# Sixteen tokens of one head in each partition of the q and k tiles, in a fused attention and feed-forward kernel

## The chip, the core and the metric

The kernel runs on one core of a Trainium2 chip. The metric is device time in microseconds (us) from launch to end; it is given as the median of several runs. One further execution was recorded by the hardware profiler, and all readings of engines, queues and waits come from that one.

## The reference

`q`, `k` and `v` are float32 of shape (8 batches, 8 heads, 576 tokens, 64). Attention is local: each chunk of 64 tokens attends to itself alone. The result, with the heads side by side, is a (4608, 512) matrix `x`, which goes through a multiplicative feed-forward.

```
chunk = 64;  scale = 1 / sqrt(64)
scores = scale * q_c @ k_c^T            # per batch, head and chunk: 64 x 64
attn   = softmax(scores)
out    = attn @ v_c                     # -> x: (4608, 512)
a = x @ w1;  b = x @ w2                 # (512 -> 1024) each
h = (a * b) @ w3                        # (1024 -> 1024)
result = h @ w_out                      # (1024 -> 512), float32
```

The kernel multiplies `w3` and `w_out` once (steps V, W, Z below) and then uses only the product `w3o`.

## The kernel before

The 4608 tokens are cut into 18 parts of 256 tokens (four chunks of 64; part number `p`), and two parts make a group of 512 (`g = p // 2`). All matmuls are in bf16. `ORDER` is one long string that writes out by hand the order of all steps; each step is a letter with its part and further numbers, and each engine runs its own steps strictly in that order. The letters that matter here:

- `R0`, `R1`: load `q` and `k` of part 0 as float32 (`raw`) on the queues of SyncE and ScalarE. `K0`, `K1`: ScalarE casts them to bf16.
- `q5`, `k5`, `v5` and so on: load part 5 with a cast from float32 to bf16 in the DMA. These, and all weights (`i0` to `i3` are quarters of `w1` and `w2`, `o` is `w_out`, `h0`, `h1` are halves of `w3`), are issued by GpSimd (POOL) on one queue, in the order of the string.
- `T p.s`: VectorE (DVE) transposes `q` (s=0) or `k` (s=1) of part `p`, in blocks of 32 x 32, from the tile `qk` to the tile `qkT` (line 201).
- `S`: scores on TensorE (PE) (64 small matmuls). `E`: exp on ScalarE. `P`: the product with `v` on PE (64 small matmuls). The tile `vbuf` holds a column of ones beside `v`, so the row sums come with it.
- `N p.u`: reciprocal and scaling on DVE. `X p.u`: transpose to `xt` (or `xm` from part 8 on) on DVE (lines 297, 305).
- `A`, `B` p.j: the products with `w1` and `w2` on PE. `C`: ScalarE copies A's result to SBUF. `M`: DVE multiplies (line 366).
- `O`, `Y`, `Q`: output product on PE, copy on ScalarE, store on SyncE's queue. `G`, `H`: from part 8 on, SBUF to SBUF moves on SyncE's queue.
- `D which.p.j.n.cols`: `n` matmuls of zeros over `cols` columns into a PSUM tile that is written properly afterwards.

PE's matmuls are all issued through one helper (line 95), POOL's loads through another (line 98), SyncE's moves through a third (line 193). PSUM is a pool of four tiles of two banks each; `qk` tiles have five buffers and `qkT` tiles two.

In `qk`, before, a partition of a 32-partition block holds two consecutive tokens of each of the 8 heads: per head a run of 2 x 64 float32 = 512 B in memory, 256 B in bf16. A block of 32 partitions is one chunk. The transpose writes, inside each 32 x 32 block, 32 elements that lie two elements (4 B) apart.

Of the kernel before, what the change touches and what calls it, by code (L numbers as in the profile page):

```python
# [7 lines left out]

ORDER = """
R0 R1 v0 q1 k1 i0 v1 i1 i2 q2 k2 v2 i3 q3 k3 v3 q4 k4 v4 o h0 h1 D0.0.0.16.64 K0 T0.0 K1 T0.1 q5 k5  # L10
v5 S0 T1.0 E0 P0 D0.1.0.4.512 T1.1 q6 k6 v6 N0.0 S1 D1.0.0.5.512 X0.0 N0.1 X0.1 A0.0 E1 B0.0 C0.0 P1
M0.0 A0.1 N1.0 X1.0 B0.1 C0.1 N1.1 A0.2 X1.1 B0.2 C0.2 M0.1 A1.0 T2.0 B1.0 C1.0 M0.2 A1.1 T2.1 q7 k7
v7 B1.1 C1.1 M1.0 S2 M1.1 A0.3 E2 T3.0 B0.3 C0.3 P2 M0.3 A1.2 N2.0 X2.0 B1.2 C1.2 N2.1 A1.3 X2.1
B1.3 C1.3 M1.2 A2.0 T3.1 q8 k8 v8 B2.0 C2.0 M1.3 S3 T4.0 A2.1 E3 M2.0 B2.1 T4.1 q9 k9 C2.1 P3 v9
M2.1 A2.2 N3.0 B2.2 C2.2 X3.0 A2.3 N3.1 B2.3 X3.1 C2.3 M2.2 S4 M2.3 A3.0 E4 B3.0 C3.0 A3.1 M3.0 B3.1
C3.1 V0 A3.2 M3.1 B3.2 C3.2 V1 A3.3 M3.2 B3.3 C3.3 V2 W0 M3.3 V3 W1 Z0 V4 V5 W2 Z1 V6 V7 T5.0 Z2 W3
T5.1 q10 k10 T6.0 T6.1 P4 v10 q11 k11 Z3 S5 N4.0 O0 E5 X4.0 N4.1 X4.1 T7.0 O1 T7.1 Y0 Q0 T8.0 P5 v11
q12 k12 Y1 S6 T8.1 O2 Q1 E6 N5.0 X5.0 N5.1 X5.1 O3 T9.0 T9.1 Y2 G4.0 P6 v12 q13 k13 A4.0 N6.0 B4.0
G4.1 Y3 X6.0 N6.1 C4.0 A4.1 X6.1 B4.1 C4.1 M4.0 Q2 S7 Q3 M4.1 A4.2 E7 T10.0 B4.2 C4.2 T10.1 P7 v13
q14 k14 A4.3 M4.2 B4.3 N7.0 C4.3 A4.4 X7.0 M4.3 B4.4 C4.4 N7.1 A4.5 M4.4 B4.5 C4.5 X7.1 S8 M4.5 S9  # L20
E8 A4.6 T11.0 B4.6 E9 T11.1 P8 v14 q15 k15 C4.6 A4.7 M4.6 G5.0 B4.7 C4.7 N8.0 A6.0 M4.7 B6.0 N8.1
C6.0 G5.1 A6.1 X8.0 B6.1 M6.0 C6.1 X8.1 P9 v15 A6.2 M6.1 N9.0 B6.2 C6.2 N9.1 A6.3 M6.2 B6.3 C6.3
X9.0 A6.4 M6.3 B6.4 C6.4 X9.1 A6.5 T12.0 H4.0 B6.5 C6.5 M6.4 A6.6 M6.5 B6.6 T12.1 H4.1 C6.6 S10 S11
M6.6 E10 A6.7 T13.0 B6.7 E11 P10 T13.1 C6.7 O4 M6.7 G6.0 N10.0 N10.1 X10.0 G6.1 P11 Y4 X10.1 O5
N11.0 N11.1 x11 q16 k16 v16 Q4 X11.0 X11.1 T14.0 A8.0 H5.0 Y5 B8.0 T14.1 C8.0 A8.1 M8.0 B8.1 H5.1
C8.1 T15.0 A8.2 B8.2 M8.1 C8.2 T15.1 Q5 A8.3 B8.3 C8.3 M8.2 G7.0 S12 M8.3 S13 E12 A8.4 T16.0 B8.4
E13 G7.1 P12 T16.1 C8.4 A8.5 B8.5 M8.4 C8.5 N12.0 A8.6 M8.5 B8.6 C8.6 N12.1 x12 q17 k17 v17 A8.7
M8.6 B8.7 C8.7 X12.0 P13 M8.7 A10.0 X12.1 B10.0 C10.0 N13.0 A10.1 M10.0 B10.1 N13.1 C10.1 A10.2
X13.0 B10.2 M10.1 C10.2 X13.1 S14 S15 M10.2 E14 A10.3 H6.0 T17.0 B10.3 E15 P14 T17.1 C10.3 A10.4
H6.1 M10.3 B10.4 C10.4 N14.0 A10.5 M10.4 B10.5 G8.0 C10.5 N14.1 A10.6 M10.5 B10.6 C10.6 X14.0 P15  # L30
G8.1 X14.1 A10.7 M10.6 B10.7 N15.0 C10.7 O6 N15.1 M10.7 X15.0 X15.1 H7.0 S16 Y6 S17 O7 E16 E17 H7.1
P16 Y7 O8 Q6 N16.0 Q7 N16.1 X16.0 X16.1 P17 Y8 A12.0 N17.0 Q8 B12.0 N17.1 C12.0 A12.1 X17.0 B12.1
M12.0 C12.1 X17.1 A12.2 M12.1 H8.0 B12.2 C12.2 A12.3 M12.2 B12.3 C12.3 H8.1 A12.4 M12.3 B12.4 C12.4
A12.5 M12.4 B12.5 C12.5 A12.6 M12.5 B12.6 C12.6 A12.7 M12.6 B12.7 C12.7 O9 M12.7 O10 Y9 Q9 A14.0 Y10
B14.0 C14.0 Q10 A14.1 M14.0 B14.1 C14.1 A14.2 M14.1 B14.2 C14.2 A14.3 M14.2 B14.3 C14.3 A14.4 M14.3
B14.4 C14.4 A14.5 M14.4 B14.5 C14.5 A14.6 M14.5 B14.6 C14.6 A14.7 M14.6 B14.7 C14.7 O11 M14.7 O12
Y11 Q11 A16.0 Y12 B16.0 C16.0 Q12 A16.1 M16.0 B16.1 C16.1 A16.2 M16.1 B16.2 C16.2 A16.3 M16.2 B16.3
C16.3 A16.4 M16.3 B16.4 C16.4 A16.5 M16.4 B16.5 C16.5 A16.6 M16.5 B16.6 C16.6 A16.7 M16.6 B16.7
C16.7 O13 M16.7 O14 Y13 Q13 O15 Y14 Q14 O16 Y15 Q15 Y16 Q16 O17
"""  # L40


# [4 lines left out]
def first_path(  # L47
# [41 lines left out]

    def inorder(ins):  # L90
        tc.keep_in_program_order(ins)
        return ins

    def mm(*a, **kw):
        return inorder(nc.tensor.matmul(*a, **kw))  # L95
# [20 lines left out]
    for t in vbuf:  # L116
        inorder(nc.vector.memset(t[:, :, :, D:W], 1.0))
# [12 lines left out]
    qk_t = {}  # L130

    HH = H // 2
    raw_t = {}

    def do_R(s):

        raw_t[s] = msb.tile([P, H, 2 * D], f32, tag="o_sb", name="raw")
        inorder((nc.sync, nc.scalar)[s].dma_start(
            raw_t[s][:], (q, k)[s][0, :, 0:4 * CH, :].rearrange("h (p t) d -> p h (t d)", t=2)))

    def do_K(s):
        if 0 not in qk_t:
            qk_t[0] = io.tile([P, 2, H, 2 * D], bf, tag="qk", bufs=5, name="qk")
        inorder(nc.scalar.copy(qk_t[0][:, s], raw_t[s][:]))  # L144
# [12 lines left out]
    def do_w(p):

# [28 lines left out]
    qkT_t, qkm_t, s_t, e_t, pv_t, xn_t, xm_t, xt_t = {}, {}, {}, {}, {}, {}, {}, {}  # L187
# [7 lines left out]
    def do_T(p, s, h=None):  # L195


        g = p // 2
        if g not in qkT_t:
            qkT_t[g] = asb.tile([P, 2, 2, 2, H, CH], bf, tag="qkT", bufs=2, name="qkT")  # L200
        inorder(nc.vector.transpose(  # L201
            qkT_t[g][:, :, p % 2, s, heads(h)].rearrange("p e h (y t) -> p h t e y", t=2),
            qk_t[p][:, s, heads(h)].rearrange("p h (t e y) -> p h t e y", t=2, e=2)))
# [34 lines left out]
    def do_P(p, hh=None):  # L238
# [183 lines left out]
    def load_q(p, h=None):
        load_qk(p, (0,), h)

    def load_k(p, h=None):
        load_qk(p, (1,), h)
# [6 lines left out]
    def load_half3(i):  # L433
# [134 lines left out]
```

## Time and profile before

| | |
|---|---|
| median of 3 runs | 244.32 us (244.03 to 244.93) |
| the profiled execution's own time | 244.48 us |
| its span, first to last instruction | 242.9 us |
| PE busy | 226.7 us (93%), 2753 matmuls |
| VectorE (DVE) busy | 154.3 us (64%), 235 instructions |
| ScalarE (ACT) busy | 85.2 us (35%) |
| GpSimd (POOL) busy | 83.7 us (34%) |
| POOL's DMA queue | 82592 packets, 18.88 MB |
| read from HBM, written to it | 38.80 MB, 9.44 MB |
| granted TensorE clock | 1.00 |

Busy time is the sum of the instructions on an engine. A window of the profile gives the busy time of each engine in a stretch of the span, with the number of instructions, then the granted clock, the DMA share and the rate at which the DMA engines moved data; for a load with a cast that rate counts the bf16 bytes that are written, half of those that are read. `L201` is line 201 of the kernel.

### The profile page before, as it was taken

The page shows a single profiled execution, that of the slowest core. Times are in us where ns is not written, and L with a number is a line of the kernel's source. Part 1 is how long each engine was busy: PE and PEld are TensorE (multiplying, and loading weights), DVE is VectorE, ACT ScalarE, POOL GpSimd, SP SyncE. Part 2 cuts the span into 40 slices and gives each one's busy share as a digit, 9 for nine tenths or more (in the row PEclk, how much of TensorE's full clock was granted, in tenths as well). Part 3 has the DMA queues.
Part 4 walks back from the last instruction along what each step waited for, and adds up shares of the span by engine and source line. Part 5 has one row for each costly group of instructions (what it writes and reads, how often), then busy time and mean ns, then how long its engine had stood idle before and what let it go on. Part 6 is the DMA issues. An engine that isn't in the chain of part 4 may idle for free.

```text
span 242.9 us, 6385 instructions
## 1 busy us (share of the span) xinstructions
PE 226.7 (93%) x2753; PEld 120.2 (49%) x2753; DVE 154.3 (64%) x235; ACT 85.2 (35%) x116; POOL 83.7 (34%) x114
## 2 busy tenths in 40 slices
PE   1189989999999999999999999999999999999994
PEld 1147868874445444444444444444444444444443
DVE  1756799699799588999998899918540332143000
ACT  2412423423333344425336234162332332322322
POOL 7856976656986345764160230000000000000000
PEclk9999999999999999999999999999999999999999
DMA  6999999999999999999999793735502200400244
GB/s 173 179 185 181 185 169 200 196 193 171 167 173 218 222 228 259 179 224 196 205 236 223 221 139 91 163 88 209 142 0 89 87 0 0 173 3 1 86 173 173
DMA packets 93597, 37.65 MB, mean 155 GB/s; under 512 B 75008, under 2 KB 86528, under 8 KB 93568
## 3 DMA queue, kind: packets, MB, share of 16 engines
q0 software_dynamic: 82592, 18.88, 83.9%
q1 hardware_dynamic: 9936, 17.83, 24.0%
q10 hardware_dynamic: 1040, 0.52, 0.8%
q8 instruction: 21, 0.34, 0.6%
q14 instruction: 8, 0.07, 0.1%
HBM read 38.80 MB, written 9.44 MB: 199 GB/s over the span
## 4 chain that ended last, share of the span: by engine, by line
PE 72%; DMA 16%; DVE 4%; SPq 3%; POOL 2%; issue 1%; ACT 0%; DVEq 0%; POOLq 0%
PE ab_ps L95 39%; PE o_ps L95 23%; PE w_ps L95 6%; DMA w<-in_moe_w_dram 4%; DMA qkm<-qkT 3%; SPq L193 3%; DMA qk<-in_q_dram 3%; DMA qk<-in_k_dram 3%; DMA xt<-xm 3%; PE pv L95 2%; PE s_ps L95 2%; DVE qkT L201 2%; POOL vbuf L98 1%; POOL w L98 1%; DVE xt L297 1%
## 5 line engine op out<-in xcount | busy, mean ns | idle before, releaser
L95 PE MATMUL ab_ps<-xt,w 128*128 128x512 bf16 (+1 forms) x688 | 127.4, 342 | 0.7 <-DVE xt L297 0.6
L95 PEld LDWEIGHTS <-w 128*128 128x128 bf16 x704 | 67.1, 98 | 56.1 <-issue 1.8
L366 DVE TENSOR_TENSOR ab<-a_sb,ab_ps 128x512 bf16<-128x512 f32 x71 | 47.8, 674 | 43.4 <-ACT a_sb L351 43.1
L351 ACT COPY a_sb<-ab_ps 128x512 f32<-128x512 f32 x71 | 41.6, 586 | 81.3 <-PE ab_ps L95 81.0
L95 PE MATMUL o_ps<-w3o,ab 128*128 128x512 bf16 (+1 forms) x296 | 63.9, 373 | 0.0
L201 DVE STREAM_TRANSPOSE qkT<-qk 128x1024 bf16<-128x1024 bf16 x36 | 45.1, 1291 | 7.2 <-ACT qk L144 5.5
L95 PEld LDWEIGHTS <-ab 128*128 128x128 bf16 x296 | 28.5, 98 | 32.2
L98 POOL DMA_DIRECT2D vbuf<-in_v_dram x40 | 33.9, 855 | 20.4 <-DMA qk<-in_q_dram 5.2
L396 ACT COPY o_sb<-o_ps 128x1024 f32<-128x1024 f32 x17 | 17.2, 1012 | 45.3 <-PE o_ps L95 41.3
L264 DVE TENSOR_TENSOR xn<-pv,rcs 128x512 bf16<-128x512 f32 x36 | 24.9, 692 | 1.4
L98 POOL DMA_DIRECT2D qk<-in_q_dram x23 | 18.1, 790 | 8.9 <-DMA qk<-in_k_dram 2.4
L98 POOL DMA_DIRECT2D qk<-in_k_dram x23 | 18.0, 783 | 6.5 <-DMA vbuf<-in_v_dram 3.7
L234 ACT ACTIVATE e<-s_ps 128x1024 bf16<-128x1024 f32 x16 | 15.9, 1026 | 1.7 <-PE s_ps L95 1.3
L95 PE MATMUL w_ps<-wo,w3T 128*128 128x512 bf16 x64 | 14.0, 379 | 0.0
L305 DVE STREAM_TRANSPOSE xm<-xn 128x512 bf16<-128x512 bf16 x20 | 13.5, 696 | 0.2
L261 DVE RECIPROCAL rcs<-pv 128x8 f32<-128x8 f32 x36 | 6.9, 193 | 10.4 <-PE pv L95 10.4
L98 POOL DMA_DIRECT2D w<-in_moe_w_dram x16 | 11.1, 695 | 5.3 <-DMA wo<-in_moe_w_out_dram 2.9
L95 PEld LDWEIGHTS <-e 64*32 64x32 bf16 (+1 forms) x832 | 7.8, 97 | 8.7 <-issue 6.9
L95 PE MATMUL pv<-vbuf,e 64*32 64x65 bf16 (+1 forms) x832 | 10.2, 197 | 1.8 <-ACT e L234 1.1
L297 DVE STREAM_TRANSPOSE xt<-xn 128x512 bf16<-128x512 bf16 x16 | 11.4, 711 | 0.5
L389 DVE COPY o_sb<-o_ps 128x256 f32<-128x256 f32 x1 | 0.4, 425 | 16.0 <-PE o_ps L95 16.0
L95 PEld LDWEIGHTS <-qkT 32*64 32x64 bf16 x512 | 5.5, 117 | 10.1 <-DVE qkT L201 7.9
(29 smaller groups left out, 54.2 us busy)
## 6 DMA issues: line engine op xcount, KB each, us to landing
out_dram<-o_sb SPq DMA_DIRECT2D x17, 512.0 KB, 3.3
qkm<-qkT SPq DMA_DIRECT2D x40, 128.0 KB, 4.0
vbuf<-in_v_dram POOLq DMA_DIRECT2D x32, 128.0 KB, 8.2
w<-in_moe_w_dram POOLq DMA_DIRECT2D x16, 256.0 KB, 9.9
qk<-in_q_dram POOLq DMA_DIRECT2D x11, 256.0 KB, 6.8
qk<-in_k_dram POOLq DMA_DIRECT2D x11, 256.0 KB, 7.8
xt<-xm SPq DMA_DIRECT2D x40, 64.0 KB, 3.2
wo<-in_moe_w_out_dram POOLq DMA_DIRECT2D x4, 256.0 KB, 7.1
```

The source lines that it names most:

```text
L95: return inorder(nc.tensor.matmul(*a, **kw))
L98: return inorder(nc.gpsimd.dma_start(dst, src))
L193: inorder(nc.sync.dma_start(dst, src))
L201: inorder(nc.vector.transpose(qkT_t[g][:, :, p % 2, s, heads(h)].rearrange("p e h (y t) -> p h t e y", t=2), qk_t[p][:, s, heads(h)].rearr ...
L234: inorder(nc.scalar.activation(e_t[p][:, :, heads(hh)], s_t[p][:].rearrange("p u (h q) -> p u h q", q=CH)[:, :, heads(hh)], Exp, scale=sca ...
L261: inorder(nc.vector.reciprocal(rc, pv[:, :, :, D:W]))
L264: inorder(nc.vector.tensor_mul(xn_t[p][:, u], pv[:, :, :, 0:D], rc.to_broadcast([P, 2, 4, D])))
L297: inorder(nc.vector.transpose(new_xt(g)[:].rearrange("p (o t) -> p o t", o=KO)[:, :, t0:t0 + UT] .rearrange("p o (m y) -> p m o y", y=BL), ...
L305: inorder(nc.vector.transpose(xm_t[g][:, u, :, m].rearrange("p o (c y) -> p c o y", y=BL), xn_t[p][:].rearrange("p u r m d -> p (u r) m d" ...
L351: inorder(nc.scalar.copy(a_t[p, j][:], ps_t[p, j][:, 0, :]))
L366: inorder(nc.vector.tensor_mul(o, view(a_t.pop((p, j))[:]), view(ps_t.pop((p, j))[:, 1, :])))
L396: inorder(nc.scalar.copy(o_sb[:], ps_t.pop(p)[:]))
```

## The change

The loads and the transpose of `q` and `k` use another placement, and the steps at the start come in another order.

```
+    RUN = 16
     # do_R: float32 tiles of part 0
-        raw_t[s] = msb.tile([P, H, 2 * D], f32, tag="o_sb", name="raw")
+        raw_t[s] = msb.tile([P, RUN * D], f32, tag="o_sb", name="raw")
-            raw_t[s][:], (q, k)[s][0, :, 0:4 * CH, :].rearrange("h (p t) d -> p h (t d)", t=2)))
+            raw_t[s][:], (q, k)[s][0, :, 0:4 * CH, :].rearrange("h (g t) d -> g h (t d)", t=RUN)))
...
     # load_qk: the casting loads of parts 1 to 17
-                load(qk_t[p][at * BL:(at + m) * BL, s, heads(h)],
-                     (q, k)[s][b, heads(h), c * CH:(c + m) * CH, :].rearrange("h (p t) d -> p h (t d)", t=2))
+                load(qk_t[p][at * BL:(at + m) * BL, s],
+                     (q, k)[s][b, :, c * CH:(c + m) * CH, :].rearrange("h (g t) d -> g h (t d)", t=RUN))
...
     # do_T
-            qkT_t[g][:, :, p % 2, s, heads(h)].rearrange("p e h (y t) -> p h t e y", t=2),
-            qk_t[p][:, s, heads(h)].rearrange("p h (t e y) -> p h t e y", t=2, e=2)))
+            qkT_t[g][:, :, p % 2, s].rearrange("p e h (g t) -> p t e g h", t=RUN),
+            qk_t[p][:, s].rearrange("p (t e y) -> p t e y", t=RUN, e=2)))
```

A block of 32 partitions is still one chunk, but its partitions are now 4 groups of 16 tokens times 8 heads; each holds one run of 16 x 64 float32 = 4 KB in memory, 2 KB in bf16. A load of 128 partitions so has 128 runs instead of 1024. `qkT` is laid out as before, so nothing after the transpose changes; inside a 32 x 32 block the transpose now writes elements that lie one head (64 elements, 128 B) apart, eight of them, then a step of 16 elements (32 B) to the next group.

The order, at the start only (from `M0.0 A0.1 N1.0 ...` on, all steps are as before):

```
before: ... S0 T1.0 E0 P0 D0.1.0.4.512 T1.1 q6 k6 v6 N0.0 S1 D1.0.0.5.512 X0.0 N0.1 X0.1 A0.0 E1 B0.0 C0.0 P1 M0.0 ...
after:  ... S0 T1.0 E0 P0 D0.1.0.4.512 D1.0.0.4.512 N0.0 X0.0 N0.1 X0.1 T1.1 q6 k6 v6 A0.0 B0.0 S1 E1 C0.0 P1 M0.0 ...
```

On DVE, `T1.1` moves behind the four steps `N0.0` to `X0.1`. On PE, `S1` moves behind `A0.0` and `B0.0`, and there is one zero matmul less (4 + 4 instead of 4 + 5), all of them now directly behind `P0`. On POOL the order of the loads stays the same.

More of the change, by code (lines that the diff above doesn't have):

```diff
@@ L9 @@
 ORDER = """
[L10 to L31, printed above, removed]
@@ L32 @@
-P16 Y7 O8 Q6 N16.0 Q7 N16.1 X16.0 X16.1 P17 Y8 A12.0 N17.0 Q8 B12.0 N17.1 C12.0 A12.1 X17.0 B12.1
+R0 R1 v0 q1 k1 i0 v1 i1 i2 q2 k2 v2 i3 q3 k3 v3 q4 k4 v4 o h0 h1 D0.0.0.16.64 K0 T0.0 K1 T0.1 q5 k5 v5
+S0 T1.0 E0 P0 D0.1.0.4.512 D1.0.0.4.512 N0.0 X0.0 N0.1 X0.1 T1.1 q6 k6 v6 A0.0 B0.0 S1 E1 C0.0 P1 M0.0
+A0.1 N1.0 X1.0 B0.1 C0.1 N1.1 A0.2 X1.1 B0.2 C0.2 M0.1 A1.0 T2.0 B1.0 C1.0 M0.2 A1.1 T2.1 q7 k7 v7 B1.1
+C1.1 M1.0 S2 M1.1 A0.3 E2 T3.0 B0.3 C0.3 P2 M0.3 A1.2 N2.0 X2.0 B1.2 C1.2 N2.1 A1.3 X2.1 B1.3 C1.3 M1.2
@@ new lines @@
+A2.0 T3.1 q8 k8 v8 B2.0 C2.0 M1.3 S3 T4.0 A2.1 E3 M2.0 B2.1 T4.1 q9 k9 C2.1 P3 v9 M2.1 A2.2 N3.0 B2.2
+C2.2 X3.0 A2.3 N3.1 B2.3 X3.1 C2.3 M2.2 S4 M2.3 A3.0 E4 B3.0 C3.0 A3.1 M3.0 B3.1 C3.1 V0 A3.2 M3.1 B3.2
+C3.2 V1 A3.3 M3.2 B3.3 C3.3 V2 W0 M3.3 V3 W1 Z0 V4 V5 W2 Z1 V6 V7 T5.0 Z2 W3 T5.1 q10 k10 T6.0 T6.1 P4
+v10 q11 k11 Z3 S5 N4.0 O0 E5 X4.0 N4.1 X4.1 T7.0 O1 T7.1 Y0 Q0 T8.0 P5 v11 q12 k12 Y1 S6 T8.1 O2 Q1 E6
+N5.0 X5.0 N5.1 X5.1 O3 T9.0 T9.1 Y2 G4.0 P6 v12 q13 k13 A4.0 N6.0 B4.0 G4.1 Y3 X6.0 N6.1 C4.0 A4.1 X6.1
@@ new lines @@
+B4.1 C4.1 M4.0 Q2 S7 Q3 M4.1 A4.2 E7 T10.0 B4.2 C4.2 T10.1 P7 v13 q14 k14 A4.3 M4.2 B4.3 N7.0 C4.3 A4.4
+X7.0 M4.3 B4.4 C4.4 N7.1 A4.5 M4.4 B4.5 C4.5 X7.1 S8 M4.5 S9 E8 A4.6 T11.0 B4.6 E9 T11.1 P8 v14 q15 k15
+C4.6 A4.7 M4.6 G5.0 B4.7 C4.7 N8.0 A6.0 M4.7 B6.0 N8.1 C6.0 G5.1 A6.1 X8.0 B6.1 M6.0 C6.1 X8.1 P9 v15
+A6.2 M6.1 N9.0 B6.2 C6.2 N9.1 A6.3 M6.2 B6.3 C6.3 X9.0 A6.4 M6.3 B6.4 C6.4 X9.1 A6.5 T12.0 H4.0 B6.5
+C6.5 M6.4 A6.6 M6.5 B6.6 T12.1 H4.1 C6.6 S10 S11 M6.6 E10 A6.7 T13.0 B6.7 E11 P10 T13.1 C6.7 O4 M6.7
@@ new lines @@
+G6.0 N10.0 N10.1 X10.0 G6.1 P11 Y4 X10.1 O5 N11.0 N11.1 x11 q16 k16 v16 Q4 X11.0 X11.1 T14.0 A8.0 H5.0
+Y5 B8.0 T14.1 C8.0 A8.1 M8.0 B8.1 H5.1 C8.1 T15.0 A8.2 B8.2 M8.1 C8.2 T15.1 Q5 A8.3 B8.3 C8.3 M8.2 G7.0
+S12 M8.3 S13 E12 A8.4 T16.0 B8.4 E13 G7.1 P12 T16.1 C8.4 A8.5 B8.5 M8.4 C8.5 N12.0 A8.6 M8.5 B8.6 C8.6
+N12.1 x12 q17 k17 v17 A8.7 M8.6 B8.7 C8.7 X12.0 P13 M8.7 A10.0 X12.1 B10.0 C10.0 N13.0 A10.1 M10.0 B10.1
+N13.1 C10.1 A10.2 X13.0 B10.2 M10.1 C10.2 X13.1 S14 S15 M10.2 E14 A10.3 H6.0 T17.0 B10.3 E15 P14 T17.1
@@ L33 @@
+C10.3 A10.4 H6.1 M10.3 B10.4 C10.4 N14.0 A10.5 M10.4 B10.5 G8.0 C10.5 N14.1 A10.6 M10.5 B10.6 C10.6
+X14.0 P15 G8.1 X14.1 A10.7 M10.6 B10.7 N15.0 C10.7 O6 N15.1 M10.7 X15.0 X15.1 H7.0 S16 Y6 S17 O7 E16 E17
+H7.1 P16 Y7 O8 Q6 N16.0 Q7 N16.1 X16.0 X16.1 P17 Y8 A12.0 N17.0 Q8 B12.0 N17.1 C12.0 A12.1 X17.0 B12.1
 M12.0 C12.1 X17.1 A12.2 M12.1 H8.0 B12.2 C12.2 A12.3 M12.2 B12.3 C12.3 H8.1 A12.4 M12.3 B12.4 C12.4
@@ L35 @@
 B14.0 C14.0 Q10 A14.1 M14.0 B14.1 C14.1 A14.2 M14.1 B14.2 C14.2 A14.3 M14.2 B14.3 C14.3 A14.4 M14.3
[L36 to L39, printed above, removed]
+B14.4 C14.4 A14.5 M14.4 B14.5 C14.5 A14.6 M14.5 B14.6 C14.6 A14.7 M14.6 B14.7 C14.7 O11 M14.7 O12 Y11
+Q11 A16.0 Y12 B16.0 C16.0 Q12 A16.1 M16.0 B16.1 C16.1 A16.2 M16.1 B16.2 C16.2 A16.3 M16.2 B16.3 C16.3
+A16.4 M16.3 B16.4 C16.4 A16.5 M16.4 B16.5 C16.5 A16.6 M16.5 B16.6 C16.6 A16.7 M16.6 B16.7 C16.7 O13
+M16.7 O14 Y13 Q13 O15 Y14 Q14 O16 Y15 Q15 Y16 Q16 O17
 """
@@ L135, in do_R @@
     def do_R(s):
-        raw_t[s] = msb.tile([P, H, 2 * D], f32, tag="o_sb", name="raw")
+        raw_t[s] = msb.tile([P, RUN * D], f32, tag="o_sb", name="raw")
         inorder((nc.sync, nc.scalar)[s].dma_start(
-            raw_t[s][:], (q, k)[s][0, :, 0:4 * CH, :].rearrange("h (p t) d -> p h (t d)", t=2)))
+            raw_t[s][:], (q, k)[s][0, :, 0:4 * CH, :].rearrange("h (g t) d -> g h (t d)", t=RUN)))
     def do_K(s):
         if 0 not in qk_t:
-            qk_t[0] = io.tile([P, 2, H, 2 * D], bf, tag="qk", bufs=5, name="qk")
+            qk_t[0] = io.tile([P, 2, RUN * D], bf, tag="qk", bufs=5, name="qk")
         inorder(nc.scalar.copy(qk_t[0][:, s], raw_t[s][:]))
@@ L147, in heads, with load_qk @@
         return slice(0, H) if h is None else slice(h * HH, (h + 1) * HH)
-    def load_qk(p, which, h=None):
+    def load_qk(p, which):
         if p not in qk_t:
-            qk_t[p] = io.tile([P, 2, H, 2 * D], bf, tag="qk", bufs=5, name="qk")
+            qk_t[p] = io.tile([P, 2, RUN * D], bf, tag="qk", bufs=5, name="qk")
         for s in which:
             for at, b, c, m in spans(4 * p, 4):
-                load(qk_t[p][at * BL:(at + m) * BL, s, heads(h)],
-                     (q, k)[s][b, heads(h), c * CH:(c + m) * CH, :].rearrange("h (p t) d -> p h (t d)", t=2))
+                load(qk_t[p][at * BL:(at + m) * BL, s],
+                     (q, k)[s][b, :, c * CH:(c + m) * CH, :].rearrange("h (g t) d -> g h (t d)", t=RUN))
     def do_w(p):
@@ L420, in do_Z, with load_q, load_k @@
         inorder(nc.scalar.copy(w3o[:, 2 * m:2 * m + 2, :], ps_t.pop(("w", m))[:]))
[L422 to L426, printed above, removed]
+    def load_q(p):
+        load_qk(p, (0,))
+    def load_k(p):
+        load_qk(p, (1,))
     def load_w12(i):
```

## The prediction

> **What bounds the kernel now.** I read the engine totals first, then the busy time by stretches of the span, then the same for the transposes alone, and last the order of instructions in the first 25 us. In the totals PE is busy for 93% of the span:
>
> ```profile
> PE 226.7 (93%) x2753; PEld 120.2 (49%) x2753; DVE 154.3 (64%) x235; ACT 85.2 (35%) x116; POOL 83.7 (34%) x114
> ```
>
> By stretches (columns: PE, PEld, DVE, ACT, POOL busy, clock, DMA share, GB/s):
>
> ```profile
> 0.00:10.00 10.00, 1.21 (x28) 1.05 (x32) 3.32 (x10) 3.27 (x3) 8.56 (x14) 1.00 1.20 172
> 10.00:25.00 15.00, 12.42 (x320) 8.90 (x315) 9.96 (x17) 3.81 (x5) 9.42 (x13) 1.00 1.75 183
> 25.00:60.00 35.00, 34.05 (x562) 25.85 (x560) 30.46 (x40) 12.65 (x18) 22.81 (x33) 1.00 1.69 187
> 60.00:100.00 40.00, 39.51 (x699) 19.50 (x698) 33.73 (x47) 15.17 (x19) 25.32 (x32) 1.00 1.80 208
> 100.00:150.00 50.00, 49.90 (x592) 23.47 (x590) 46.11 (x73) 20.55 (x30) 17.09 (x23) 1.00 1.40 195
> ```
>
> From 25 us on PE rests for 1.0 us of 35, then 0.5 of 40 and 0.1 of 50, so whatever a faster load gives there is worth almost nothing. There are two other things to see. PE's idle time lies in the first 25 us (8.8 + 2.6 us), and DVE has little room: its idle time is 4.5 us between 25 and 60, 6.3 us between 60 and 100, and 3.9 us between 100 and 150. The transposes of q and k alone (L201; busy, count) take this much of DVE:
>
> ```profile
> 25.00:60.00 35.00, 7.60 (x6) 1.00 1.69 187
> 60.00:100.00 40.00, 17.02 (x14) 1.00 1.80 208
> 100.00:150.00 50.00, 15.11 (x12) 1.00 1.40 195
> ```
>
> So the change pulls at two ends: the loads, whose gain can be felt only at the start, and a DVE instruction that occurs 32 times where DVE is nearly full.
>
> **The start.** The timeline shows what PE waits for (start, duration):
>
> ```profile
> 6.21 1.99 ACT L144 CAST qk<-raw 128x1024 bf16<-128x1024 f32 x2 [3.45 <-DMA raw<-in_q_dram]
> 7.29 5.32 DVE L201 STREAM_TRANSPOSE qkT<-qk 128x1024 bf16<-128x1024 bf16 x4 [5.50 <-ACT qk L144]
> 9.82 1.07 PE L95 MATMUL z_ps<-qkT 32*64 32x64 bf16 x64 [7.36 <-DVE qkT L201]
> ...
> 12.02 0.75 PE L95 MATMUL pv<-vbuf,e 64*32 64x65 bf16 x64 [1.13 <-ACT e L234]
> ...
> 12.71 1.89 PE L95 MATMUL z_ps<-zero 128*128 128x512 bf16 x4
> ...
> 18.51 1.25 PE L95 MATMUL z_ps<-xt,w 128*128 128x256 bf16 x10 [1.12 <-issue]
> ```
>
> The raw q lands at 6.2 us; the two casts follow, then T0.0 and T0.1, and S0 can start at 9.82.
>
> Term 1, the raw loads. They move 1.05 MB, of which q comes first. A window from 3 to 5 us reads 309 GB/s, when both are under way in runs of 512 B. The best that the cast loads reach further on, below, is 204 GB/s written, 408 GB/s read. At these two rates 1.05 MB takes 3.4 or 2.6 us, so k gains up to 0.8 us, and q between nothing (if q and k now share the engines evenly from the first packet) and about 1.3 us. I take 0.8 us for S0, nearer the row for 309, since the fixed part of the 5.2 us to landing does not change.
>
> Term 2, the queue of POOL. Three windows, each of a load with another run:
>
> ```profile
> 8.00:10.00 2.00, 0.18 (x12) 0.18 (x16) 1.93 (x3) 0.21 (x1) 1.85 (x3) 1.00 1.82 181
> 17.00:20.00 3.00, 1.88 (x56) 1.36 (x54) 0.00 (x0) 0.20 (x1) 1.36 (x2) 1.00 1.46 195
> 38.50:41.50 3.00, 3.00 (x87) 2.51 (x86) 3.00 (x5) 1.45 (x2) 1.50 (x3) 1.00 1.23 204
> ```
>
> By the order of the queue these are q1 and k1 (256 B written per run), w1 and w2 (512 B) and w_out (1 KB): 181, 195, 204 GB/s. Eight times fewer packets therefore do not mean eight times less time; runs of 2 KB should go at 204 or slightly above. The five loads up to q3 (1.31 MB written) then take 6.4 instead of 7.2 us. The chain of waits runs through q3, which DVE waits 1.3 us for at 30.6 us; what PE waits for DVE's xt behind it is 0.6 us in two places. I count 0.5 us of this as gain; the bounds are 0 and 0.6. [...]
>
> Term 3, the order. Between the end of P0 (12.77) and A0.1 (20.32) PE spent 7.55 us. Now it does 8 zero matmuls (the first four took 0.47 us each, the other five 0.25): 2.9 to 3.8 us, which also covers the 3.0 us that N0 and X0 needed from the end of P0. Then come A0.0 and B0.0 (1.92), S1 (0.65 to 1.02), a wait for E1 that nothing on PE hides any more (S0 to P0: 1.13), and P1 (0.63 to 0.75). That makes 7.2 to 8.6 us. The 1.12 us marked "issue" in the middle of B0.0 is waiting for nothing shown; it comes again, goes, or falls into the wait for E1. The bounds are -0.3 and +2.2 us; I take +0.1, near the lower end, with the 1.12 us falling into E1's wait. Behind the moved T1.1 on DVE stands M0.0, which waits for C0.0 anyway; q6 to v6 keep their places on POOL.
>
> Term 4, POOL's issuing: a q or k issue takes 0.79 us, one of w_out (256 runs) 0.58, so 46 issues become perhaps 0.2 us shorter each. POOL runs ahead and waits for buffers; zero.
>
> Term 5, the transpose. The rows by form (count, busy, mean ns):
>
> ```profile
> L201 DVE STREAM_TRANSPOSE qkT<-qk 128x1024 bf16<-128x1024 bf16 x36 | 45.1, 1291 | 7.2 <-ACT qk L144 5.5 <-DMA qk<-in_q_dram 1.3
> L305 DVE STREAM_TRANSPOSE xm<-xn 128x512 bf16<-128x512 bf16 x20 | 13.5, 696 | 0.2
> L407 DVE STREAM_TRANSPOSE w3T<-w 128x1024 bf16<-128x1024 bf16 x8 | 9.6, 1223 | 1.0 <-DMA w<-in_moe_w_dram 0.8 <-PE w_ps L95 0.3
> L117 DVE MEMSET vbuf<- 128x16 bf16 x6 | 0.4, 72 | 0.0
> ```
>
> L407 writes 32 elements side by side, L201 one every 4 B, L305 reads one every 8 B: all go at about one element per ns. Nothing here writes one every 128 B except, remotely, the memset of the ones column, 16 elements 160 B apart in 72 ns: 4.5 ns each at most, since a fixed cost is in it. So the new transpose lies between 1.22 and 4.6 us. I take 1.3, the nearest transpose rows, and zero cost.
>
> The sum of the forecast: 244.5 (this execution's own 244.48; its span is 242.9, and the median of the runs is 0.16 lower) - 0.8 - 0.5 + 0.1 = 243.3. Its own range is 241.8 to 245.0.
>
> **The rivals.**
>
> *The strided write halves DVE's rate* (slower). Place: L201. Price: 1024 elements by the slope between L407 and L305 (1223 - 696 over 512, 1.03 ns) is 1.05 us per transpose, so 2.3 us. Two of them stand on the chain to S0: +2.1. Beyond 25 us the extra is 6.3, 14.7 and 12.6 us in the three stretches against idle time of 4.5, 6.3 and 3.9, leaving 1.8, 8.4 and 8.7. Together +21 us; less the forecast's gain, 264 to 265; if none of the idle time can be filled, 279. I take 266. It begins to decide where 12 transposes use up 3.9 us, at about 1.6 us each. For it: DVE's rooms are small, and the nearest row with such steps is the memset. Against it: steps of 4 and 8 B cost under 6%. [...]
>
> *Something between*: L201 over L407 is 68 ns for a step of 4 B instead of 2; if each further doubling up to 128 B costs as much, the transpose takes 1.6 us, and half way from there to half rate 1.95. At 1.95 the extra of 0.65 leaves 2.8 us (60 to 100) and 3.9 us (from 100 on) over the idle time, and 1.3 at the start: 8 us. So 244 to 251.
>
> *Four ns an element*: 4.6 us each; 3.3 x 34 - 14.7 is +97 us, 342.
>
> *The new order costs*: the E1 wait and the 1.12 us do not overlap, term 3 is +2.2, while terms 1 and 2 give less; 245.8.
>
> *Nothing happens*: the DMA cuts the runs up again, or the loads hide behind others; 244.4.
>
> **How the numbers follow.** Forecast 0.46, half rate 0.28, in between 0.12, four ns 0.05, order 0.06, nothing 0.03. A measurement of this kernel can tell about 0.5%, 1.2 us. The forecast sits at this border: 0.24 faster, 0.20 same, 0.02 slower. From the others: in between 0.03 same and 0.09 slower; order 0.01 same and 0.05 slower; nothing 0.01 faster and 0.02 same; half rate and four ns slower. In total 0.25 faster, 0.26 same, 0.49 slower. The range must reach to the half-rate case and leaves the four-ns case out: 241.6 to 268.
>
> **What would show it.** L201's mean: near 1.3 us (forecast), 1.6 to 2, 2.3 or 4.6. Right at the start: the cast of raw at 5.4 instead of 6.2, S0 at 9.0, a PE gap of about 1.1 us before P1, A0.1 at or below 19.7. POOL's queue: about 30000 packets fewer, and no q3 wait on DVE at 30 us. If PE shows waits for DVE between 60 and 150 us, the forecast is wrong; if S0 is early and A0.1 is not, term 3 is.

## The result, and the profile after

The changed kernel takes 362.58 us (median of 4 runs, 362.42 to 364.81) against 244.51 us for the kernel before in the same session: a ratio of 1.485, 95% interval 1.479 to 1.492. It is 118 us slower, far above the predicted range. The profiled execution took 362.64 us, with a span of 361.1 us.

The engine totals, the granted clock over the span in 40 slices, and the packet total of the changed kernel:

```profile
PE 255.4 (71%) x2752; PEld 129.4 (36%) x2752; DVE 274.1 (76%) x235; ACT 85.2 (24%) x116; POOL 74.4 (21%) x114
PEclk9997869599996959969698879588969999999999
DMA packets 62877, 37.65 MB, mean 104 GB/s; under 512 B 41728, under 2 KB 51200, under 8 KB 62848
```

DVE has the same 235 instructions and is busy for 274.1 instead of 154.3 us; PE's share fell from 93% to 71%. By stretches (columns as in the prediction's table: PE, PEld, DVE, ACT, POOL busy, clock, DMA share, GB/s):

```profile
25.00:60.00 35.00, 23.20 (x400) 18.22 (x399) 31.69 (x26) 7.21 (x11) 21.56 (x34) 0.80 1.50 193
60.00:100.00 40.00, 33.04 (x432) 21.17 (x432) 37.45 (x28) 10.19 (x13) 7.28 (x10) 0.87 0.60 64
100.00:150.00 50.00, 30.12 (x479) 13.44 (x480) 49.53 (x30) 8.87 (x10) 13.81 (x21) 0.83 0.66 98
```

From 25 to 150 us DVE rests for 6.3 us and PE for 38.6: the two have changed places, DVE is the bound. The rows of DVE up to 264 us, when the last transpose of `k` ends, show which instruction it is (count, busy, mean ns, then the idle time ahead of it with its releaser):

```profile
L201 DVE STREAM_TRANSPOSE qkT<-qk 128x1024 bf16<-128x1024 bf16 x36 | 167.1, 4794 | 7.4 <-ACT qk L144 7.4
L366 DVE TENSOR_TENSOR ab<-a_sb,ab_ps 128x512 bf16<-128x512 f32 x43 | 32.0, 753 | 8.6 <-ACT a_sb L351 8.6
...
L261 DVE RECIPROCAL rcs<-pv 128x8 f32<-128x8 f32 x28 | 5.9, 210 | 0.0
```

One transpose takes 4794 ns instead of 1291. Now the account. In the kernel before the last of these transposes ends at 148.3 us, in the changed one at 264.0; each span is cut there, first before, then after:

```profile
0.00:148.30 148.30, 135.38 (x2174) 78.00 (x2175) 122.10 (x179) 54.87 (x73) 83.19 (x112) 1.00 1.61 195
148.30:243.00 94.70, 91.34 (x581) 42.18 (x578) 32.20 (x57) 30.34 (x43) 0.53 (x2) 1.00 0.29 92
```

```profile
0.00:264.00 264.00, 162.26 (x2176) 86.95 (x2177) 241.86 (x179) 55.50 (x74) 73.88 (x112) 0.85 0.78 110
264.00:361.00 97.00, 93.15 (x576) 42.43 (x575) 32.27 (x58) 29.73 (x42) 0.54 (x2) 0.97 0.27 88
```

Up to the cut DVE's busy time grew by 241.86 - 122.10 = 119.8 us, and its idle time went from 26.2 only to 22.1 us: 119.8 - 4.1 = 115.7. The rest grew by 2.3 us, at a granted clock of 0.97. Together that is the 118.

The start of the changed kernel, by its timeline (start, duration, and in brackets the idle time before):

```profile
8.12 1.99 ACT L144 CAST qk<-raw 128x1024 bf16<-128x1024 f32 x2 [5.18 <-DMA raw<-in_q_dram]
9.19 13.79 DVE L201 STREAM_TRANSPOSE qkT<-qk 128x1024 bf16<-128x1024 bf16 x3 [7.40 <-ACT qk L144]
18.48 1.07 PE L95 MATMUL z_ps<-qkT 32*64 32x64 bf16 x64 [16.01 <-DVE qkT L201]
```

The cast begins 1.9 us later than before (6.21), not 0.8 earlier, and S0 starts at 18.48 instead of 9.82: 1.9 of that is the load and nearly all of the rest is two slow transposes. The issues of the two raw loads (size, us to landing) show why the cast is late:

```profile
raw<-in_k_dram ACTq DMA_DIRECT2D x1, 512.0 KB, 4.7
raw<-in_q_dram SPq DMA_DIRECT2D x1, 512.0 KB, 7.1
```

`k` lands first, `q` 2.4 us after it, and the kernel wants `q` first. In the trace the packets of `k` run from 2.40 to 4.70 us and those of `q` only from 4.40 to 6.97, one load after the other; in the kernel before `q`'s run from 2.10 to 5.59 and `k`'s from 3.41 to 6.39. Why `k`'s come first now was not tried.

### The profile page after: what moved, and what is told of

Same layout as the page of the kernel before. It is cut to its first block, busy times and chain, and to the rows that moved or that the text cites. A ratio compares the mean times of both kernels' runs of the same rounds, so it can differ in the third digit from the quotient of the medians.

```text
span 361.1 us, 6384 instructions
## 1 busy us (share of the span) xinstructions
PE 255.4 (71%) x2752; PEld 129.4 (36%) x2752; DVE 274.1 (76%) x235; ACT 85.2 (24%) x116; POOL 74.4 (21%) x114
## 2 busy tenths in 40 slices
DMA packets 62877, 37.65 MB, mean 104 GB/s; under 512 B 41728, under 2 KB 51200, under 8 KB 62848
## 4 chain that ended last, share of the span: by engine, by line
DVE 52%; PE 37%; issue 5%; DMA 3%; ACT 1%; SPq 1%; DVEq 0%
DVE qkT L201 42%; PE ab_ps L95 23%; PE o_ps L95 12%; DVE ab L366 4%; DVE xn L264 3%; DMA raw<-in_q_dram 2%; DVE xt L297 2%; PE w_ps L95 2%; SPq L193 1%; DVE xm L305 1%; PE pv L95 1%; ACT a_sb L351 1%; DMA qkm<-qkT 1%; DVE rcs L261 0%; ACT qk L144 0%
## 5 line engine op out<-in xcount | busy, mean ns | idle before, releaser
L201 DVE STREAM_TRANSPOSE qkT<-qk 128x1024 bf16<-128x1024 bf16 x36 | 167.1, 4794 | 7.4 <-ACT qk L144 7.4
L95 PE MATMUL ab_ps<-xt,w 128*128 128x512 bf16 (+1 forms) x688 | 145.8, 376 | 32.8 <-DVE ab L366 30.1
L95 PEld LDWEIGHTS <-w 128*128 128x128 bf16 x704 | 73.2, 106 | 100.3 <-issue 46.6
L366 DVE TENSOR_TENSOR ab<-a_sb,ab_ps 128x512 bf16<-128x512 f32 x71 | 51.2, 726 | 48.1 <-ACT a_sb L351 48.1
L95 PE MATMUL o_ps<-w3o,ab 128*128 128x512 bf16 (+1 forms) x296 | 71.4, 403 | 16.1 <-DVE xn L264 16.1
L95 PEld LDWEIGHTS <-ab 128*128 128x128 bf16 x296 | 30.0, 104 | 54.4 <-DVE xn L264 17.2
L98 POOL DMA_DIRECT2D qk<-in_q_dram x23 | 13.1, 573 | 46.6 <-DVE qkT L201 35.8
L95 PE MATMUL z_ps<-qkT 32*64 32x64 bf16 x128 | 1.8, 216 | 18.7 <-DVE qkT L201 18.7
L95 PE MATMUL s_ps<-qkT 32*64 32x64 bf16 x384 | 5.0, 208 | 13.7 <-DVE qkT L201 11.5
L305 DVE STREAM_TRANSPOSE xm<-xn 128x512 bf16<-128x512 bf16 x20 | 13.5, 696 | 0.2
L98 POOL DMA_DIRECT2D qk<-in_k_dram x23 | 12.7, 554 | 3.8 <-DMA w<-in_moe_w_dram 3.2
```

What stands on the lines that cost most here:

```text
L201: inorder(nc.vector.transpose(qkT_t[g][:, :, p % 2, s].rearrange("p e h (g t) -> p t e g h", t=RUN), qk_t[p][:, s].rearrange("p (t e y) -> ...
L305: inorder(nc.vector.transpose(xm_t[g][:, u, :, m].rearrange("p o (c y) -> p c o y", y=BL), xn_t[p][:].rearrange("p u r m d -> p (u r) m d" ...
L366: inorder(nc.vector.tensor_mul(o, view(a_t.pop((p, j))[:]), view(ps_t.pop((p, j))[:, 1, :])))
```

## The experiments

Two questions were open. Is it the transpose alone, and what in it? And what are the loads and the order worth without it? Where a kernel permutes what `qkT` holds, its amount of work stays the same.

**One part at a time.** Three kernels. The first has the changed kernel's loads and order, but a transpose that writes side by side:

```
 after.py, do_T
-  qkT_t[g][:, :, p % 2, s].rearrange("p e h (g t) -> p t e g h", t=RUN),
+  qkT_t[g][:, :, p % 2, s].rearrange("p e h c -> p e (h c)").rearrange("p e (t y) -> p t e y", t=RUN),
```

> The changed kernel, but the transpose of q and k writes its 32 elements side by side (no step of 128 B). This leaves out the right placement in qkT, so the scores are of other pairs. Loads, reads of the transpose and order are as in the changed kernel. Theory 1, the write step is the whole cost: L201 back to 1.2 to 1.3 us, the time is what the forecast meant, 242.5 to 246 (the raw load of q now lands 1.9 us later, which the forecast had wrong). Rival 2, the 4 KB runs or the read side of the transpose slow it: L201 stays near 4.8 us, time near 360. Rival 3, half of the loss is PE's lower clock or the new order: L201 near 1.3, but time above 250.

It takes 245.42 us, ratio 1.0035 (1.0008 to 1.0061), at a granted clock of 1.00, so the changed kernel's lower clock comes with the slow write too. Its row of the transposes:

```profile
L201 DVE STREAM_TRANSPOSE qkT<-qk 128x1024 bf16<-128x1024 bf16 x36 | 42.6, 1216 | 7.3 <-ACT qk L144 7.2
```

The second is the kernel before with only the 128 B write steps of the change:

```
 before.py, do_T
-  qkT_t[g][:, :, p % 2, s, heads(h)].rearrange("p e h (y t) -> p h t e y", t=2),
-  qk_t[p][:, s, heads(h)].rearrange("p h (t e y) -> p h t e y", t=2, e=2)))
+  qkT_t[g][:, :, p % 2, s].rearrange("p e h (g t) -> p t e g h", t=16),
+  qk_t[p][:, s].rearrange("p h (t e y) -> p (h t) e y", t=2, e=2)))
```

> The kernel before, with its own loads and its own order; only the transpose writes with the changed kernel's pattern (eight elements 128 B apart, four such groups). This leaves out the right placement in qkT. Theory 1: L201 at 4.7 to 4.9 us and time at 355 to 365, nearly all of the loss without any change of the loads. Rival 2: L201 near 1.3 us, time near 245. If the time is well below 355 with L201 at 4.8, the order and the loads add to it.

361.26 us, ratio 1.4751 (1.4705 to 1.4798):

```profile
L201 DVE STREAM_TRANSPOSE qkT<-qk 128x1024 bf16<-128x1024 bf16 x36 | 166.9, 4800 | 5.7 <-ACT qk L144 5.7
```

So the write pattern alone makes 116.7 us; the whole change made 118. The third is the kernel before with the changed kernel's `ORDER`, and nothing else:

```
 before.py
- ... D0.1.0.4.512 T1.1 q6 k6 v6 N0.0 S1 D1.0.0.5.512 X0.0 N0.1 X0.1 A0.0 E1 B0.0 C0.0 P1 ...
+ ... D0.1.0.4.512 D1.0.0.4.512 N0.0 X0.0 N0.1 X0.1 T1.1 q6 k6 v6 A0.0 B0.0 S1 E1 C0.0 P1 ...
```

> The kernel before with the changed kernel's order of steps and nothing else. Term 3 of the prediction: between -0.3 and +2.2 us, taken as +0.1. Rival (the order is part of the loss): more than +2.2.

244.61 us, ratio 0.9994 (0.9982 to 1.0005). The order costs nothing: P1 waits 1.14 us for E1, and the 1.12 us gap marked "issue" in B0.0 is gone.

**What in the write is slow.** Behind the kernel before, two passes of extra DVE and ACT instructions, each on 1024 elements per partition, which differ in the step of the write or the read. Their sum is in the run's time; only the single durations are of use.

```
 before.py, behind the last step (two passes of 18 such lines; at(t, s): 32 elements, s elements apart)
+  inorder(nc.vector.transpose(at(dst, 1), inp(1)))      # steps of 2 B
+  inorder(nc.vector.transpose(at(dst, 2), inp(2)))      # 4 B
...
+  inorder(nc.vector.transpose(at(dst, 64), inp(64)))    # 128 B
...
+  inorder(nc.scalar.copy(dst[:, 0:4096].rearrange("p (a s) -> p s a", s=64)[:, 0:16], ...))
```

> The kernel before with a tail, twice over, behind its last step: transposes of 128x1024 bf16 that write steps of 2, 4, 8, 16, 32, 64, 128, 256 and 132 B, two that read steps of 128 and 16 B and write side by side, and copies on DVE and ACT with and without steps. The output is unchanged. Theory 1a, one element per 16-byte line is slow, however far the lines: 1.2 us up to a step of 8 B, 4.7 us from 16 B on, 132 B like 128 B, and reads with steps likewise. Theory 1b, half rate: 2.3 us from 16 B on. Theory 1c, a collision of steps that are powers of two: rising with the step, 132 B as fast as 2 B. Theory 1d, the pattern's short inner loop of eight: all of these near 1.2 to 1.3 us, since their inner loop is 32.

From the timeline of the first pass (start, duration): writes in steps of 2, 4, 8, 16, 128 and 132 B, then a read in steps of 128 B with a dense write, then ScalarE's copy with a write step of 128 B:

```profile
241.18 1.19 DVE L460 STREAM_TRANSPOSE w<-w 128x1024 bf16<-128x1024 bf16 x1
242.40 1.31 DVE L461 STREAM_TRANSPOSE w<-w 128x1024 bf16<-128x1024 bf16 x1
243.74 2.44 DVE L462 STREAM_TRANSPOSE w<-w 128x1024 bf16<-128x1024 bf16 x1
246.21 4.70 DVE L463 STREAM_TRANSPOSE w<-w 128x1024 bf16<-128x1024 bf16 x1
...
260.09 4.73 DVE L466 STREAM_TRANSPOSE w<-w 128x1024 bf16<-128x1024 bf16 x1
...
269.62 4.68 DVE L468 STREAM_TRANSPOSE w<-w 128x1024 bf16<-128x1024 bf16 x1
274.33 1.89 DVE L469 STREAM_TRANSPOSE w<-w 128x1024 bf16<-128x1024 bf16 x1
...
285.44 4.74 ACT L477 COPY w<-w 128x1024 bf16<-128x1024 bf16 x1
```

The duration nearly doubles from a step of 4 to 8 B and again to 16 B, and then stays, up to 256 B (4.45 to 4.73 us). A step of 132 B costs what 128 B does (4.68 us against 4.73), so it is no collision of a power of two. All of these write 32 elements in their inner loop, so the short loop of eight is not the cause either. A read with a wide step costs 1.89 us, a write 4.7. ScalarE pays as much (its dense copy takes 1.04 us), so it is not a matter of the transpose. DVE's bf16 copy shows the same rise at half the price: 0.43 us dense, 0.74 in steps of 4 B, 2.45 at 128 B. A second set of extra lines asks whether the step counts or the size of what is written in one piece:

```
 before.py, behind the last step (two passes of 14 such lines)
+  inorder(nc.vector.transpose(apart(dst, 16, 128, 2, 32), ...))   # pairs (4 B), then a step of 512 B
...
+  inorder(nc.vector.transpose(fd[:].rearrange("p (y s) -> p s y", s=32), ...))   # float32, steps of 128 B
```

> The kernel before with another tail, twice over. bf16 transposes that write 2, 4 or 8 neighbours (4, 8, 16 B) and then step 512, 1024 or 2048 B; float32 transposes and copies with and without steps of 32 and 128 B; bf16 copies on DVE and ACT with steps of 8, 4 and 32 B. The output is unchanged. Theory A, each new 16-byte line costs a write about 4.6 ns: 2.3 us for pairs, 1.2 to 1.3 us for fours and eights, and float32 with a step of 128 B at 4.7 us on ACT and in the transpose. Theory B, a write narrower than 4 B costs 4.6 ns by itself unless it merges with its neighbour: pairs at 1.2 to 1.3 us already, float32 at 128 B without any loss (near the dense time).

The float32 transpose, dense and in steps of 128 B, ScalarE's float32 copy in steps of 128 B, and the bf16 transpose that writes pairs far apart:

```profile
245.26 1.20 DVE L462 STREAM_TRANSPOSE fd<-fs 128x1024 f32<-128x1024 f32 x1
246.50 1.91 DVE L463 STREAM_TRANSPOSE fd<-fs 128x1024 f32<-128x1024 f32 x1
252.48 2.02 ACT L470 COPY fd<-fs 128x1024 f32<-128x1024 f32 x1
258.76 1.25 DVE L459 STREAM_TRANSPOSE w<-w 128x1024 bf16<-128x1024 bf16 x1 [3.88 <-ACT w L472]
```

Pairs of bf16 elements, 512 B apart, go at nearly full speed (1.25 us; dense 1.19). Four bytes that stand alone (float32) take 1.9 us instead of 1.20, two bytes that stand alone 4.7. Neither theory came out whole: A had 2.3 us for the pairs and 4.7 for float32, B had no loss for float32. What decides for bf16 in these rows is not the step as such: pairs 512 B apart cost next to nothing extra, while lone elements cost the transpose 2.4 ns each in steps of 8 B (2.44 us / 1024) and 4.3 to 4.6 ns from 16 B on (4.45 to 4.73 us / 1024). ScalarE's copy is close to that, 2.46 us in steps of 8 B and 4.74 at 128 B; DVE's copy takes about half of it, 1.30 and 2.45 us. Why a lone two-byte write costs that was not tried, and stays open.

**Between the ends.** The kernel before with a write step of 8 B, to test how a transpose of 2.4 us turns into time, the ground of the half-rate rival:

```
 before.py, do_T
-  qkT_t[g][:, :, p % 2, s, heads(h)].rearrange("p e h (y t) -> p h t e y", t=2),
+  qkT_t[g][:, :, p % 2, s].rearrange("p e h c -> p e (h c)").rearrange("p e (n y f) -> p n f e y", y=BL, f=4),
   (and the blocks of qk read in that order)
```

> The kernel before, the transpose of q and k writing steps of 8 B (placement in qkT left out): 2.44 us each by the sweep instead of 1.29. It tests the prediction's arithmetic of the half-rate rival, idle time of DVE against extra time, on its own: 1.15 us extra each gives 2.4 + 9.8 + 9.9 us over the idle time in the three stretches and 2.3 at the start, 269 us; with no idle time filled 284. If a wait on PE's side or a lower clock adds to it, it is above 269; if DVE's own order lets more be hidden, below.

274.02 us, ratio 1.1182 (1.1134 to 1.1230); the transposes take 2453 ns. By the account used above, cut where the last of them ends (178.1 us), DVE's busy time grows by 160.15 - 122.10 = 38.05 us and its idle time falls by 8.25, to 17.95, so 29.8 us are seen; the rest of the span is as before (94.8 us). The time lies above the 269 us that were expected, because 8.25 us of idle time were filled and not 14.7.

**The raw loads.** Both kernels have the dense write. The first takes `k` ahead of `q`, the second loads `raw` in 512 B runs as before and keeps 4 KB runs for the casting loads:

```
 the first kernel of this section, ORDER
- ... D0.0.0.16.64 K0 T0.0 K1 T0.1 ...
+ ... D0.0.0.16.64 K1 T0.1 K0 T0.0 ...
```

```
 the first kernel of this section, do_R (the cast reads the same 1024 elements)
-  raw_t[s][:], (q, k)[s][0, :, 0:4 * CH, :].rearrange("h (g t) d -> g h (t d)", t=RUN)))
+  raw_t[s][:], (q, k)[s][0, :, 0:4 * CH, :].rearrange("h (p t) d -> p h (t d)", t=2)))
```

> The run with the dense write, and K1 T0.1 ahead of K0 T0.0. Leaves out the right placement in qkT as that one does. There k's raw tile came first and q's last (7.96 us), while ScalarE cast q first, so S0 started at 11.46. Theory (the loss of that run, about 0.9 us, is the order in which the raw tiles land): S0 at 10.3, time 1.1 us lower, 244.2 to 244.5. Rival (4 KB runs cost elsewhere, or the loads that are now faster are hidden anyway): S0 earlier, time unchanged at 245.4.

> The run with the dense write, but the raw tiles of part 0 are loaded in 512 B runs as in the kernel before (their placement is not put right). What is left of the change are the casting loads in 4 KB runs and the order. Term 2 of the prediction said 0.5 us gain for these (0 to 0.6), term 3 +0.1: 243.9 to 244.6, S0 near 9.8. Rival (the faster loads gain nothing or cost): 244.6 to 245.4.

With `k` first: 244.59 us, ratio 0.9988 (0.9970 to 1.0006), the cast of `k` at 5.97, of `q` at 8.32 us, S0 at 10.69. With short raw runs: 243.87 us, ratio 0.9963 (0.9945 to 0.9980), the cast at 6.15, S0 at 9.65. With the dense write alone S0 was at 11.46. Against their kernels before, the dense write is 0.8 us slower, with `k` first level (0.1 faster, which is not clear of the noise), with short raw runs 0.8 faster (by the interval 0.5 to 1.3). So the long runs of the casting loads (with the order, which is worth nothing, and a transpose that is 0.07 us shorter) gain 0.8 us, long runs of the raw loads lose about 1.6, and taking `k` first gets about 0.9 of that back; the last two are differences of such differences, uncertain by about 0.8 us. S0 moves alike, by 1.8 and 0.8 us.

**A whole version with long runs.** To write pairs or more, the heads go innermost in `qkT`; then PE reads its operand with a step. First all 8 heads, so that PE's step is 16 B, with `k` first:

```
 after.py
-  qkT_t[g] = asb.tile([P, 2, 2, 2, H, CH], bf, tag="qkT", bufs=2, name="qkT")
+  qkT_t[g] = asb.tile([P, 2, 2, 2, CH, H], bf, tag="qkT", bufs=2, name="qkT")
...
-  lhsT=qkT_t[g][blk[i], e, m, 1, h, :], rhs=qkT_t[g][blk[i], e, m, 0, h, :],
+  lhsT=qkT_t[g][blk[i], e, m, 1, :, h], rhs=qkT_t[g][blk[i], e, m, 0, :, h],
...
   (the transpose and the tile qkm alike; K1 T0.1 stand ahead of K0 T0.0)
```

> A whole version with the 4 KB runs: qkT holds the eight heads of a token side by side (heads innermost), so the transpose of q and k writes eight neighbours (16 B) and then steps 256 B; PE reads its operands for the scores with a step of 16 B. K1 T0.1 stand ahead of K0 T0.0. Theory (two-byte writes that stand alone are the cost): L201 at 1.25 us, the score matmuls as before (64 in 0.63 to 0.65 us), time like the run with k first, 244.0 to 244.9, no better than the kernel before. Rival 1: PE pays for its step, the 18 x 64 score matmuls and their weight loads take up to double: +6 to +12 us. Rival 2: the groups of eight still cost: L201 at 2 us or more, above 255.

262.93 us, ratio 1.0741 (1.0715 to 1.0768). The transposes are at 1219 ns, and PE pays in their place: it is busy for 244.7 instead of 226.7 us, and the kernel takes 18.2 us longer, more than the 6 to 12 us of the first rival. The scores of one part, in this kernel and then in the kernel before:

```profile
42.52 2.17 PE L95 MATMUL s_ps<-qkT 32*64 32x64 bf16 x64
```

```profile
44.29 0.74 PE L95 MATMUL s_ps<-qkT 32*64 32x64 bf16 x64
```

The weight loads from `qkT` take 210 instead of 117 ns each. The next kernel is the same, with each raw load cut into two of 2 KB runs:

```
 the kernel above, do_R
+  for c in range(2):   # tokens 0-7, then 8-15 of each run
...
-  raw_t[s][:], (q, k)[s][0, :, 0:4 * CH, :].rearrange("h (g t) d -> g h (t d)", t=RUN)))
+  raw_t[s][:, t0 * D:t1 * D], (q, k)[s][0, :, 0:4 * CH, :].rearrange("h (g t) d -> g h t d", t=RUN)[:, :, t0:t1] ...
```

> The version with heads innermost, and each raw tile of part 0 loaded by two DMAs of half a row (2 KB runs). Theory (the raw loads in 4 KB runs are slower because each engine has only eight pieces of one DMA in hand): both tiles land about 0.5 us earlier, time 0.3 to 0.6 us below the other version, 243.6 to 244.4. Rival (rate or fixed cost of the queue sets it): no earlier than 7.9 us, same time.

263.48 us, ratio 1.0758 (1.0733 to 1.0784): the cutting gains nothing. Compared with the version before it, the tiles do not land earlier: the last packet of `k` ends at 5.83 us instead of 4.73, that of `q` at 7.54 instead of 6.93. The edit also did something that was not meant: ScalarE's table load (ACT_TABLE_LOAD in the trace, 1.28 us), which ran at 1.66 us while the loads were under way, now waits for `k` until 6.76, so the casts start only at 8.05 and S0 at 11.56 instead of 10.45. Last, only two heads innermost: pairs for DVE's write, a step of 4 B for PE's read, and two transposes of 512 elements per tile:

```
 after.py
-  qkT_t[g] = asb.tile([P, 2, 2, 2, H, CH], bf, tag="qkT", bufs=2, name="qkT")
+  qkT_t[g] = asb.tile([P, 2, 2, 2, HH, CH, 2], bf, tag="qkT", bufs=2, name="qkT")
...
+  for e in range(2):
+      qkT_t[g][:, e, p % 2, s].rearrange("p h (g t) w -> p t g h w", t=RUN),
+      qk_t[p][:, s].rearrange("p (t e y) -> p t e y", t=RUN, e=2)[:, :, e]))
   (S reads [..., h // 2, :, h % 2]; K1 T0.1 stand ahead of K0 T0.0)
```

> A whole version with the 4 KB runs: qkT holds two heads of a token side by side, so the transpose (now two of 512 elements, one for each half of the head's 64) writes pairs (4 B) and then steps, and PE reads the scores' operands with a step of 4 B instead of 16 B. K1 T0.1 ahead of K0 T0.0. Theory (pairs write at full rate; PE's loss comes from a step of 16 B): L202 at 0.68 to 0.72 us, 64 score matmuls in 0.65 us, time 244.2 to 245.2, level with the kernel before. Rival 1 (PE pays for any step): 64 score matmuls above 1 us, 250 or more. Rival 2 (pairs cost in the real pattern): L202 at 1.2 us, 265 or more.

244.04 us, ratio 0.9973 (0.9956 to 0.9990). Its transposes, and the scores of one part:

```profile
L202 DVE STREAM_TRANSPOSE qkT<-qk 128x512 bf16<-128x512 bf16 x72 | 45.0, 678 | 6.5 <-ACT qk L144 6.3 <-DMA qk<-in_q_dram 0.2
```

```profile
38.05 0.71 PE L95 MATMUL s_ps<-qkT 32*64 32x64 bf16 x64
```

DVE's sum is that of the kernel before (45.1 us), and PE's read costs nothing extra. So the placement of the change can be had, and with `k` first it is worth 0.6 us, 0.3% (0.1 to 0.4%). Pairs together with short raw runs were not run.

## Why the prediction was wrong

**Term 5 failed, and it is nearly all of the error.** It put the transpose between 1.22 and 4.6 us and took 1.3 and zero cost, since the transposes of the trace stood nearer to it than the memset. It took 4.79 us, above even the upper end, and the write pattern alone makes 116.7 of the 119.3 us between forecast and result. But the series it leaned on, dense, 4 B and 8 B, was not one of writes: L407 and L201 write dense and in steps of 4 B, while L305's 8 B are a step of its read, and its write is dense. The write first doubles at just those 8 B (2.44 us), beyond the last write step that the trace held. The upper end was right in size by chance: a memset of 256 four-byte values takes 272 ns and one of 1024 takes 912 (in the sweep kernel), 0.83 ns a value with 59 ns fixed, so by this estimate the 72 ns of the 16-element memset are mostly fixed cost and no 4.5 ns an element.

**The rival was named, and mispriced in chance.** "Four ns an element" is what happened. It got 0.05, and the range was allowed to leave it out although it was the stated upper bound of the term.

**Its price, 342 us, was 20.6 us low.** DVE's extra was 119.8 us instead of 3.3 x 34 = 112.2 (7.6 of it), mostly because there are 36 transposes: the price left out the two of part 1, 6.6 us at 3.3 each. Then, 14.7 us of idle time were to be filled; 4.1 were (10.6). The rest of the span added 2.3. Which idle time stayed can be read from the rows. These are the multiplications and the reciprocals of the kernel before, up to its cut:

```profile
L366 DVE TENSOR_TENSOR ab<-a_sb,ab_ps 128x512 bf16<-128x512 f32 x43 | 28.6, 666 | 6.3 <-ACT a_sb L351 6.3
L261 DVE RECIPROCAL rcs<-pv 128x8 f32<-128x8 f32 x28 | 5.3, 191 | 4.3 <-PE pv L95 4.3
```

In the changed kernel the wait ahead of the reciprocals is gone (0.0), and so is the 1.3 us for q3, but the one ahead of the multiplications grew to 8.6. Up to the first transpose of part 2 DVE's idle time is as before (11.8 us against 11.7), so none of the four transposes ahead of it was hidden, where the price counted two. In the strict order a transpose delays PE's scores and, behind them, the product that the next multiplication waits for; this wait moves with the transpose and is not used up by it. That reading is argued from the rows; the kernel with 8 B steps, where 8.25 of 38.05 us were hidden, shows the same shortfall and not its cause.

**Half rate belongs to a step of 8 B.** The half-rate rival, 266 us, put the transpose at 2.3 us. The sweep has about that in steps of 8 B (2.44 us, twice the dense 1.19); from 16 B on, lone bf16 writes take 4.4 to 4.7 us, about four times the dense time. Wide reads (1.89 us) and lone float32 writes (1.91 us, 128 B apart) cost 1.6 times the dense time.

**Term 1 failed in sign.** It expected the raw load 0.8 us earlier, from a rate that would rise from 309 to 408 GB/s; between 3 and 5 us the changed kernel moved 281, and the cast came 1.9 us later. The bound "q and k share the engines evenly" had the right question, but not the answer that `k` could land whole ahead of `q`. Long raw runs cost about 1.6 us.

**Terms 2, 3 and 4 held.** The POOL queue writes 205 GB/s with 2 KB runs (21 to 23 us in the changed kernel; 181 with 256 B), "at 204 or slightly above"; the kernel with short raw runs gains 0.8 us, with 0.5 expected from this term and at most 0.15 from the two shorter transposes at the start, and in it DVE's wait for q3 fell from 1.32 to 0.62 us. The order alone is worth 0.0 (0.1 expected). A `q` issue takes 0.57 instead of 0.79 us, and nothing shows it. The packets fell by 93597 - 62877 = 30720, as told.

## What to carry to other kernels

When an edit changes where an engine writes, look at how many neighbouring bytes each write leaves. Here pairs of bf16 elements with a wide step cost next to nothing (1.25 us against 1.19 dense; tried in the transpose alone). Single bf16 elements 16 B or more apart cost about four times as much or more: 4.4 to 4.7 us against 1.19 in the transpose, 4.74 against 1.04 in ScalarE's copy and 2.45 against 0.43 in DVE's copy, both at 128 B. Single float32 elements 128 B apart cost 1.5 to 2 times as much: 1.91 us against 1.20 in the transpose, 2.02 against 1.04 in ScalarE's copy and 1.04 against 0.69 in DVE's copy. The reader of such a layout has its own limit, here PE's: the 64 score matmuls are free at a step of 4 B (0.71 us against 0.74 dense) and take threefold at 16 B (2.17 us). And if the trace has no row like the new access, its upper bound belongs in the range, above all when the instruction stands 36 times on an engine with little room.

## What the runs showed of the hardware

- A transpose of 1024 bf16 elements per partition takes 1.2 us if it writes dense or in pairs 512 B apart, 1.31 in steps of 4 B, 2.44 at 8 B and 4.4 to 4.7 from 16 B on; 1.9 with a wide step on the read. One of 1024 float32 takes 1.2 us dense and 1.9 with lone writes, 128 B apart.
- PE's 64 score matmuls take 2.17 us with an operand step of 16 B, 0.71 with 4 B and 0.74 dense.
- In the changed kernel the two raw loads of 512 KB in 4 KB runs, on two queues, land one after the other (`k` 4.7 and `q` 7.1 us after their issue), the one that is wanted first last.
- In the changed kernel the granted clock was 0.80 to 0.87 between 25 and 150 us, where PE rested for 17 to 40% of the time, and 0.97 from 264 us on. In the kernel before it was 1.00 in every stretch shown, also in the first 10 us, where PE rests for 8.8. What of the 118 us the lower clock costs was not separated.
